# Pooled q and k of two batches summed from transposed tiles, local outputs parked in DRAM, first loads issued by two engines

## The chip, the cores and the metric

The kernel runs on one core of a Trainium2 chip. Its time is device microseconds of one execution, the median of several runs. The core has TensorE (PE in the profile: matmuls, with weight loads as PEld), VectorE (DVE), ScalarE (ACT), GpSimd (POOL) and SyncE (SP, which issues DMAs here; ScalarE can issue them too). All of them run their own instruction streams in program order and wait for one another by semaphores.

## What is computed

Three stages follow each other, all in fp32. B, H, S, D = 4, 8, 576, 64; x has 2304 tokens of 512 columns.

```
q_d, k_d, v_d = mean over 4 neighbouring tokens           # pooled: 144 tokens
out_up    = repeat(softmax(q_d k_d^T / 8) v_d, 4)          # pooled attention, back to 576 tokens
out_local = softmax(q k^T / 8 where |i - j| < 4) v         # banded attention
x = (out_up + out_local) as 2304 x 512
h = x @ w_in;  y = (h * cos(h)) @ w_out                    # first mixture, 2048 wide
yn = y / rms(y) * rms_g
out = (silu(yn @ w_gate) * (yn @ w_val)) @ w_out2          # second mixture, 1536 wide
```

## The kernel before

Every large matrix product is made of three products of rounded parts (a high and a low part of each operand), so TensorE runs at its fp32r rate; ScalarE rounds the high part and VectorE or GpSimd subtracts it to get the low part. The first mixture takes x in nine tiles of 256 tokens. A tile has sixteen chunks of w_in and w_out; two chunks of a tile are a unit (`unit`, L1054 to L1115: matmuls h in L1076, the cosine in L1094 to L1101, high and low part in L1110 to L1112), and `second` (L1142) multiplies by w_out. Units of the tiles 0 and 1 alternate. There are three places for x tiles (`xt`): tile t + 3 can be filled when tile t has been used. Weights come in pieces of 512 KB and are unpacked on ScalarE, VectorE and GpSimd (`w_conv`, L318 to L329).

The attention is the front of this, batch by batch. Of each batch, `block` (L688) does five blocks of 116 tokens for all heads: transposes of q and k (L704), scores with a band mask (L744, L750), softmax (L759 to L772), transposes (L786), the product with v (L812), then the pooled output is added from two PSUM banks, one of each half of the heads (L825), and high and low part go into the x tile (L838, L840). Tokens of the last x tile go to DRAM instead (L844). A block keeps a token `blk` (three of them) and tiles of the five scratch tiles `b2` until its end, and before L812 it waits for the pooled output `od` of its batch.

The pooled attention (`pooled`, L573, a head pair at a time) needs the sums of q, k and v over four tokens. For batch 0 they are made by matmuls from the blocks' own loads (`sums`, L414; `vsums`, L443). For batches 1 to 3, `pq_part` (L500) loads q and k again in ten pieces through a ring `pq`, sums them on GpSimd (L381, L383), transposes the sums (L522) and copies them out (L399, L401); v is loaded and summed in `pv` (L547).

The order of all instructions is worked out by a planner (`Order`, L58 to L191) when the program is built: each step is a generator that yields an engine and an estimated duration, waits for events and takes places from pools; the step that can start earliest goes next, and among those within 0.1 us the one with the smaller due time. The constants in L24 to L55 are such due times and estimates. Where TensorE would be idle in the first 215 us the planner fills in matmuls that compute nothing (`keep_warm`, L241 to L253). What runs on each engine, and in which order, is then fixed.

The start (`start`, L910) sets the order of the first loads by `LOADS` (L40): four weight pieces, five pairs of q and k (q by SP in L861, k by ScalarE in L922, as a step of its own that takes its turn among ScalarE's work), five times the four parts of v (L873, SP), four weight pieces.

Of the kernel before, what the change touches and what calls it, by code (L numbers as in the profile page):

```python
# [194 lines left out]
def fused_kernel(ctx: ExitStack, tc, q, k, v, w_in, w_out, w_gate, w_val, w_out2, rms_g, mask, bmask, out):  # L195
# [20 lines left out]
    for n, c in (("t", 2), ("kk", 2), ("g", 2), ("xt", 3), ("raw", NRAW), ("cv", NCV),  # L216
                 ("blk", 3), ("T", 1), ("blk0", 2), ("b2", 5), ("rq", NQK), ("vb", NV), ("od", 2), ("E", 1), ("qs", NQS), ("vh", 2)):
# [152 lines left out]
    def pq_tiles(b):  # L370

        PQ[b] = [ap.tile([128, 4, 144], F32, tag=f"pqs{w}", name="pqs") for w in range(2)]
# [127 lines left out]
    def pq_part(b):  # L500
# [5 lines left out]
        for w, c, x, m in parts:  # L506
            n = UC[c][1]
            if x == 0:
                qi = yield take("qs")
                qs = ap.tile([128, 4, 64], F32, tag=f"qs{qi}", name="qs")  # L510
# [12 lines left out]
            give("qs", qi)  # L523
# [4 lines left out]
        done(("pq", b))  # L528

# [17 lines left out]
    def pv(b, hp):  # L547
# [3 lines left out]
        p = []  # L551
        for _ in range(2):
            x = yield take("pq")
            p.append(x)
        t = (ap.tile([128, 512], F32, tag=p[0], name="v4").rearrange("p (c x) -> p c x", c=2),
             ap.tile([128, 512], F32, tag=p[1], name="v4")[:, :256])
# [11 lines left out]
        for x in p:  # L568
            give("pq", x)
# [3 lines left out]
    def pooled(b, hp, E=None):  # L573
# [47 lines left out]
        A = ap.tile([128, 3, 144], F32, tag=x, name="at")  # L621
# [66 lines left out]
    def block(b, u, raw, pools):  # L688
# [9 lines left out]
        for w in range(2):  # L698
# [14 lines left out]
            f = (0.125, 1.0)[w]  # L713
# [5 lines left out]
            give("att", "att")  # L719
        qt, kt = T[0][1], T[1][1]  # L720
# [3 lines left out]
        else:  # L724
            if u % 2 == 0:
# [26 lines left out]
        for x, _ in T:  # L752
            give("b2", x)
# [11 lines left out]
        ACT.activation(out=E, in_=E, func=ACTF.Exp)  # L765
# [39 lines left out]
        S_.cur["own"] = held[0][1][:, 0]  # L805
# [47 lines left out]
    def od_free(b):  # L853
        yield wait(("bo", b))
        give("od", od_i[b])

    def raw_dma(t, src, b, u):

        r0 = geo(u)[2]
        yield "SP", 1.75  # L860
# [1050 lines left out]
```

## Time and profile before

| | us |
|---|---|
| median of 3 runs (lowest to highest) | 975.62 (974.25 to 975.81) |
| the profiled execution's own time | 975.6 |
| its span, first to last instruction | 973.8 |
| TensorE busy | 957.8 |
| VectorE busy | 719.7 |
| ScalarE busy | 542.8 |
| GpSimd busy | 254.1 |

The busy times overlap, since the engines run beside each other. A busy TensorE counts the fillers as well. The mean granted TensorE clock of the execution is 0.996.

### The profile page before, as it was taken

Reading aid. Unit: us, or ns where it says so; the run is one execution under the profiler, and the core shown is the slowest. Engines: PE = TensorE matmul, PEld = TensorE weight load, DVE = VectorE, ACT = ScalarE, POOL = GpSimd, SP = SyncE. Lnnn points to the kernel's source line nnn. Section 1 sums busy time; section 2 is a strip of 40 time slices with the busy share of each in tenths; the row PEclk is TensorE's granted clock in tenths of the full one; section 3 lists DMA queues with packets and bytes.
Section 4 is the critical chain, followed back from the end, with each engine's and each line's share of the span. In section 5 each row is a group of like instructions: output and inputs, shape, how many; then the busy total and the mean of one; then the engine's idle time right before and its main releaser. Section 6 shows DMA issues by size and latency. Waiting matters only on the chain.

```text
span 973.8 us, 19223 instructions
## 1 busy us (share of the span) xinstructions
PE 957.8 (98%) x7194; PEld 884.3 (91%) x7194; DVE 719.7 (74%) x1459; ACT 542.8 (56%) x1091; POOL 254.1 (26%) x301
## 2 busy tenths in 40 slices
PE   9989989999999999999999999999999999999998
PEld 9879879888888898888888889999999999999998
DVE  4789985478757866568586789586666678999885
ACT  3667888487768756648565565233223335454432
POOL 3277578345443501100061341000000015200000
PEclk9999999999999999999999999999999999999999
DMA  9649634576796555445432211233222243444432
GB/s 204 201 98 295 177 87 130 150 193 169 206 232 175 152 167 157 146 155 206 152 123 77 74 44 53 62 93 98 82 71 78 63 152 123 142 159 151 132 119 77
DMA packets 157678, 132.16 MB, mean 136 GB/s; under 512 B 71824, under 2 KB 131600, under 8 KB 157584
## 3 DMA queue, kind: packets, MB, share of 16 engines
q1 hardware_dynamic: 152384, 129.61, 44.8%
q10 hardware_dynamic: 5200, 1.31, 0.7%
q8 instruction: 57, 0.93, 0.4%
q14 instruction: 37, 0.30, 0.1%
HBM read 94.71 MB, written 36.18 MB: 134 GB/s over the span
## 4 chain that ended last, share of the span: by engine, by line
PE 84%; DVE 9%; ACT 2%; SPq 2%; issue 2%; DMA 1%; DVEq 0%; ACTq 0%
PE gvp L1565 26%; PE y L1142 18%; PE h L1076 16%; PE o L1818 13%; PE bav L812 2%; PE btr L704 1%; SPq L861 1%; PE bs L750 1%; PE yt L1470 1%; PE avp L648 1%; DVE rawwa L324 1%; PE sps L592 1%; DMA rawwa<-in_moe_w_out 1%; DVE bt L825 1%; PE bat L786 1%
## 5 line engine op out<-in xcount | busy, mean ns | idle before, releaser
L1565 PE MATMUL gvp<-xc,wc 128*128 128x384 f32 x1296 | 231.3, 335 | 0.0
L1565 PEld LDWEIGHTS gvp<-xc,wc 128*128 128x128 f32 x1296 | 225.5, 188 | 0.2
L1636 DVE TENSOR_TENSOR tmp<-gvp,tmp 128x384 f32<-128x384 f32 x180 | 99.3, 554 | 55.3 <-PE gvp L1565 52.0
L1076 PE MATMUL h<-big,wwa 128*128 128x256 f32 (+1 forms) x756 | 124.8, 317 | 2.9 <-DVE t L1101 2.2
L1076 PEld LDWEIGHTS h<-big,wwa 128*128 128x128 f32 x756 | 107.5, 190 | 13.2 <-DVE t L1101 2.7
L1818 PE MATMUL o<-wo,wc 128*128 128x256 f32 x972 | 118.4, 279 | 0.0
L1818 PEld LDWEIGHTS o<-wo,wc 128*128 128x128 f32 x972 | 115.7, 190 | 0.0
L1142 PE MATMUL y<-wwa,big 128*128 128x512 f32 x432 | 109.5, 399 | 0.0
L1142 PEld LDWEIGHTS y<-wwa,big 128*128 128x128 f32 x432 | 78.6, 188 | 16.8 <-issue 0.8
L1096 DVE SCALAR_TENSOR_TENSOR t<-kk,h 128x512 f32<-128x512 int32 x72 | 49.1, 682 | 45.9 <-ACT kk L1094 45.7
L1076 PE MATMUL h<-big,wwb 128*128 128x256 f32 (+1 forms) x504 | 82.9, 316 | 0.0
L1142 PE MATMUL y<-wwb,big 128*128 128x512 f32 x324 | 81.0, 397 | 0.0
L1076 PEld LDWEIGHTS h<-big,wwb 128*128 128x128 f32 x504 | 72.1, 190 | 6.4 <-issue 0.2
L1094 ACT ACTIVATE kk<-h 128x512 int32<-128x512 f32 x72 | 42.7, 593 | 58.0 <-PE h L1076 57.9
L1142 PEld LDWEIGHTS y<-wwb,big 128*128 128x128 f32 x324 | 59.2, 188 | 12.2 <-issue 0.4
L1101 DVE TENSOR_TENSOR t<-h,t 128x512 f32<-128x512 f32 x72 | 49.3, 686 | 23.2 <-ACT t L1099 22.8
L1702 POOL TENSOR_TENSOR wt<-wo 128x256 f32<-128x256 f32 x10 | 9.7, 975 | 208.5 <-DMA wo<-wfs 183.1
L1099 ACT ACTIVATE t<-t,cst 128x512 f32<-128x512 f32 x72 | 51.9, 721 | 15.1 <-DVE t L1096 14.6
L1627 ACT ACTIVATE tmp<-gvp 128x384 f32<-128x384 f32 x36 | 17.7, 492 | 75.2 <-PE gvp L1565 73.0
L1761 ACT ACTIVATE wc<-ut 128x512 fp32r<-128x512 f32 (+1 forms) x60 | 34.3, 584 | 42.2 <-DVE ut L1747 25.2
L1110 ACT ACTIVATE big<-t 128x512 fp32r<-128x512 f32 x72 | 45.1, 628 | 17.6 <-DVE t L1101 17.2
L1672 DVE TENSOR_TENSOR tmp<-tmp 128x384 f32<-128x384 f32 x72 | 43.7, 608 | 11.9 <-ACT tmp L1660 11.4
(192 smaller groups left out, 1729.8 us busy)
## 6 DMA issues: line engine op xcount, KB each, us to landing
us<-tmp SPq DMA_DIRECT2D x72, 192.0 KB, 2.0
uf<-us SPq DMA_DIRECT2D x48, 256.0 KB, 2.9
rawwa<-in_moe_w_out SPq DMA_DIRECT2D x22, 512.0 KB, 4.4
wfs<-rawwa SPq DMA_DIRECT2D x36, 256.0 KB, 2.6
rawwa<-in_moe_w_gate SPq DMA_DIRECT2D x12, 512.0 KB, 4.6
rawwa<-in_moe_w_val SPq DMA_DIRECT2D x12, 512.0 KB, 4.6
wf<-wfs SPq DMA_DIRECT2D x12, 512.0 KB, 4.2
rawwa<-in_moe_w_in SPq DMA_DIRECT2D x11, 512.0 KB, 5.6
```

The costliest lines, as they stand in the source:

```text
L1076: PE.matmul(h[:, w_ * ci:w_ * ci + w_], a[:, ksl], x_at(x, kk), start=m == 0, stop=m == 11)
L1094: ACT.activation(out=kk, in_=h, func=ACTF.Copy, scale=INV2PI, bias=0.25)
L1096: DVE.scalar_tensor_tensor(out=t, in0=kk, scalar=TWOPI, in1=h, op0=ALU.mult, op1=ALU.subtract)
L1099: ACT.activation(out=t, in_=t, func=ACTF.Sin, scale=-1.0, bias=cst[:, 0:1])
L1101: DVE.tensor_tensor(out=t, in0=h, in1=t, op=ALU.mult)
L1110: ACT.activation(out=gh, in_=t, func=ACTF.Copy)
L1142: PE.matmul(y[j][b], g[:, tsl], a, start=(first and ci == 0 and i == 0), stop=(last and c == 15 and i == 2))
L1565: PE.matmul(bank, w[:, a, kk], xc[:, x, b, kk], start=first and i == 0, stop=i == 5, skip_group_check=True)
L1636: DVE.tensor_tensor(out=half(o), in0=a, in1=half(b), op=ALU.add)
L1672: DVE.tensor_tensor(out=half(v), in0=half(v), in1=half(sl), op=ALU.mult)
L1761: ACT.activation(out=o[:, 0], in_=src, func=ACTF.Copy)
L1818: PE.matmul(b[m][1][:, l], u[0][x][:, j, l], w[:, y, k], start=(p == 0 and l == 0 and i == 0), stop=(p == C3 - 1 and i == 2), skip_group_c ...
```

## The change

- For the third and the fourth batch, q and k are no longer loaded a second time for the pooled attention. When a block has transposed its q and k, `token_sums` sums four neighbouring columns of the transposed tile on VectorE, straight into the pooled tile; the transposed tile is given back when both this and the scores are done. The factor of q changes from 1/8 to 1/128 to suit both uses, and the local softmax's exponential scales by 16. Only the second batch still goes through `pq_part`; its ring has two tiles (`pqs01`, `pqs11`, which later hold the third batch's sums), and its sums take a scratch tile `b2`. The summed v has tiles of its own.
- The product of a block with v goes to one PSUM bank for both halves of the heads, and one instruction takes it out. For the first batch this adds the pooled output as before. For the others it is a plain copy (ScalarE or VectorE), stored to DRAM (`loc`), and the block ends there without having waited for the pooled output. A new step `join` waits for the pooled output and for the x tile's place, loads the parked block, adds the pooled output (GpSimd or VectorE) and goes on as before (`to_x`). The low part there may be taken by VectorE too.
- ScalarE issues the five k loads of the first batch at the very start, and one half of each v load (ten DMAs). SP issues the other ten. Three weight pieces go ahead of q instead of four, and five follow v.
- The constants of the planner (due times, biases, estimates) change.

```diff
-PH = 50
-BD = (-40, -45)
+D1 = (-170, -260, -40)
+DJ, BU = (-200, 4)
+BD = (-200, -45)
-RAWT = 1.8
-SD, PD, VD = (-200, -20, -20)
-LOADS = (("w", 4), ("r", 5), ("v", 5), ("w", 4),)
+RAWT = 1.1
+SD, PD, VD = (-40, -200, -20)
+LOADS = (("w", 3), ("r", 5), ("v", 5), ("w", 5),)
+KACT, VACT = 5, (0, 1, 2, 3, 4)
+XLB = 0.3
-SLACK = 2.5
+SLACK = 2
-DS = 0
+DS = 2
-TP = 5
-WD = 0.004
-NQS = 1
+TP = 8
+WD = 0.005
-DU = {"conv": 20, "pool": -320, "blk": -170}
+DU = {"conv": 20, "pool": -300, "blk": -200}
...
-    S_.pool("ax", ["pq1"])
-    S_.pool("pq", ["pq0", "pq2"])
+    S_.pool("pq", ["pqs01", "pqs11"])
...
+    def token_sums(b, u, w, x, o):
+        yield wait(("pq", 1) if b == 2 else ("pS", 1))
+        if b not in PQ:
+            pq_tiles(b)
+        _, n, _, off = geo(u)
+        yield "DVE", 0.6
+        DVE.tensor_reduce(out=PQ[b][w][:, :, 29 * u:29 * u + n // 4], in_=o[:, :, off:off + n].rearrange("p a (j r) -> p a j r", r=4), axis=AX.X, op=ALU.add)
+        count(("pq", b), 10)
+        if count2(("Tu", b, u, w), 2):
+            give("b2", x)
...
-            f = (0.125, 1.0)[w]
+            f = (2.0 ** -7, 1.0)[w]
...
+            if b > 1:
+                S_.add(token_sums(b, u, w, x, o), S_.cur["due"], slack=0.0)
...
-        ACT.activation(out=E, in_=E, func=ACTF.Exp)
+        ACT.activation(out=E, in_=E, func=ACTF.Exp, scale=16.0)
...
-        yield wait(("od", b))
-        held = []
-        for e in range(2):
-            yield take("att", 1 - e)
-            i = yield take("bank")
-            held.append((i, bank_tile(i, [128, 4, 116], "bav")))
+        if b < 1:
+            yield wait(("od", b))
+        yield take("att")
+        i = yield take("bank")
+        bav = bank_tile(i, [128, 4, 116], "bav")
...
-                    PE.matmul(held[e][1][pr, a, 58 * s:58 * s + m], VB[v_i][pr, s, a], ba[pr, a, 64 * s:64 * s + m], start=True, stop=True)
+                    PE.matmul(bav[pr, a, 58 * s:58 * s + m], VB[v_i][pr, s, a], ba[pr, a, 64 * s:64 * s + m], start=True, stop=True, skip_group_check=True)
...
+        if b:
+            _, e = yield [("ACT", 0.58, t0), ("DVE", 0.64, t0, None, 0.3)]
+            if e == "ACT":
+                ACT.activation(out=bx, in_=bav[:, :, :n], func=ACTF.Copy)
+            else:
+                DVE.tensor_copy(out=bx, in_=bav[:, :, :n])
...
+        if b:
+            yield "SP", 0.8
+            SP.dma_start(loc[b, u, :, :4 * n], bx.rearrange("p a q -> p (a q)"))
+            give("b2", x_i, S_.now())
+            give("blk", 0)
+            done(("loc", b, u), S_.now())
+            S_.add(join(b, u), T0 + T1 * (S * b + i0) / TT + DJ)
+            return
...
+    def join(b, u):
+        i0, n, _, _ = geo(u)
+        yield wait(("loc", b, u))
+        yield wait(("od", b))
+        for ti in range((S * b + i0) // TT, min(NTILE - 2, (S * b + i0 + n - 1) // TT) + 1):
+            yield wait(("xt", ti))
+        x_i, bx = yield from t2k()
+        bx = bx[:, :4 * n].rearrange("p (a q) -> p a q", a=4)
+        yield "SP", 0.8
+        SP.dma_start(bx.rearrange("p a q -> p (a q)"), loc[b, u, :, :4 * n])
+        _, e = yield [("POOL", 1.2), ("DVE", 0.66, None, None, 0.5)]
+        y = bx.rearrange("p a (j r) -> p a j r", r=4)
+        (POOL if e == "POOL" else DVE).tensor_tensor(out=y, in0=y, in1=pooled_at(b, i0, n), op=ALU.add)
+        count(("bo", b), 5)
+        yield from to_x(b, u, bx)
...
+    def v_act(u, x):
+        for s in range(2):
+            yield "ACT", 0.38
+            v_window(0, u, x, 0, s, ACT)
+        S_.cur["t"] += 3.5
+        count(("rv", 0, u), 2)
...
     def blk_due(b, u):
         if b == 0:
             return T0 + BD[0] if u < 3 else T0 + T1 + BD[1]
-        return T0 + T1 * (S * b + 116 * u) / TT + DU["blk"]
+        if b == 1:
+            return T0 + T1 * (S * b + 116 * u) / TT + D1[0]
+        return T0 + T1 * S * b / TT + BU * u + DU["blk"]
...
+        rt = [early(("raw", u), [128, 2, H, D]) for u in range(5)]
+        for u in range(KACT):
+            yield "ACT", 0.38, (0, None)
+            ACT.dma_start(rt[u][:, 1], k[0, :, geo(u)[2]:geo(u)[2] + 128, :].rearrange("h t d -> t h d"))
...
-                yield from load_v(0, u, x)
+                if u in VACT:
+                    S_.add(v_act(u, x), -250.0)
+                yield from load_v(0, u, x, (1,) if u in VACT else (0, 1))
```

## Rows read from the trace of the kernel before

**Rows 1.** The page's head: span, then each engine's busy us, share and instructions.

```profile
span 973.8 us, 19223 instructions
PE 957.8 (98%) x7194; PEld 884.3 (91%) x7194; DVE 719.7 (74%) x1459; ACT 542.8 (56%) x1091; POOL 254.1 (26%) x301
```

**Rows 2.** Groups by line and shape: busy us, mean ns | idle before; the fillers.

```profile
L253 PE MATMUL warm<-ident 128*128 128x128 f32 x198 | 28.2, 295 | 1.4 <-POOL ident masks.py:199 1.4
```

**Rows 3.** Busy us of each engine by stage, over the first 500 us.

```profile
core 0: us, PE busy (x) PEld busy (x) DVE busy (x) ACT busy (x) POOL busy (x), PEclk, DMA share, GB/s
0.00:24.00 24.00, 22.63 (x210) 22.13 (x210) 10.84 (x25) 9.52 (x21) 9.32 (x18) 1.00 0.92 203
0.00:14.00 14.00, 12.64 (x99) 12.64 (x99) 6.23 (x17) 5.98 (x12) 7.48 (x16) 1.00 0.91 232
14.00:34.00 20.00, 19.75 (x225) 18.69 (x224) 8.70 (x19) 8.44 (x20) 3.65 (x3) 1.00 0.77 145
34.00:56.00 22.00, 19.68 (x268) 15.85 (x266) 19.29 (x49) 16.87 (x58) 7.24 (x8) 0.92 0.50 169
80.00:140.00 60.00, 55.60 (x459) 48.83 (x458) 54.92 (x86) 51.13 (x89) 44.83 (x46) 1.00 0.65 186
140.00:200.00 60.00, 59.70 (x514) 53.42 (x513) 32.44 (x60) 42.03 (x90) 35.19 (x45) 1.00 0.46 128
200.00:500.00 300.00, 299.26 (x2404) 258.94 (x2403) 209.46 (x434) 204.81 (x395) 82.20 (x112) 1.00 0.59 175
```

**Rows 4.** Timeline, all engines, 0 to 40 us: start, us, engine, line, [idle before].

```profile
14.75 17.80 SPq L873 DMA_DIRECT2D vb<-in_v  x20
...
22.22 0.40 ACTq L922 DMA_DIRECT2D raw<-in_k  x1
...
22.72 0.67 ACT L326 ACTIVATE wwa<-rawwb 128x512 fp32r<-128x512 f32 x1 [5.08 <-DMA vb<-in_v]
...
29.64 0.97 PE L426 MATMUL pq<-sel,raw 128*128 128x28 f32 x8
```

**Rows 5.** Timeline of TensorE, 48 to 82 us: the first units, and four transposes.

```profile
62.75 4.87 PE L1076 MATMUL h<-big,wwa 128*128 128x256 f32 x36
67.46 0.60 PE L522 MATMUL trq<-ident,qs 128*64 128x128 f32 x4
67.82 1.67 PE L1076 MATMUL h<-big,wwa 128*128 128x256 f32 x12
```

**Rows 6.** Groups of VectorE by line and shape, whole span.

```profile
L825 DVE TENSOR_TENSOR bt<-bav,od 64x464 f32<-64x464 f32 x32 | 20.4, 638 | 5.8 <-PE bav L812 5.2
...
L767 DVE TENSOR_REDUCE bst<-bt 128x8 f32<-128x512 f32 x15 | 10.2, 681 | 5.7 <-ACT bt L765 5.6
```

**Rows 7.** Timeline of VectorE, 50 to 75 us.

```profile
56.45 3.99 DVE L825 TENSOR_TENSOR bt<-bav,od 64x464 f32<-64x464 f32 x6 [0.64 <-PE bav L812]
```

**Rows 8.** Timeline of TensorE, 36 to 48 us: 64-row matmuls.

```profile
38.77 1.20 PE L592 MATMUL sps<-pqs 64*72 64x144 f32 x16
...
46.14 1.69 PE L652 MATMUL avp<-at,vs 64*64 64x144 f32 x24
```

**Rows 9.** Instructions on the tile trq: duration ns min/median/max, first and last start.

```profile
L522 PE MATMUL trq<-ident,qs x54: 270/272/299, 67.5 to 296.9; 128*64 128x128 f32 x54
```

**Rows 10.** Busy us by stage, columns as in rows 3.

```profile
52.50:56.00 3.50, 3.50 (x68) 2.90 (x64) 2.46 (x5) 3.43 (x8) 1.67 (x2) 0.51 0.02 5
```

**Rows 11.** Timeline of TensorE, 118 to 192 us.

```profile
119.70 1.21 PE L592 MATMUL sps<-pqs 64*72 64x144 f32 x8
...
159.72 0.71 PE L592 MATMUL sps<-pqs 64*72 64x144 f32 x8
...
173.98 0.90 PE L648 MATMUL avp<-at,vh 128*128 128x144 f32 x6
...
190.98 1.20 PE L1076 MATMUL h<-big,wwa 128*128 128x256 f32 x8
```

**Rows 12.** The chain that ended last: start us, us, what; a block's product.

```profile
176.26 1.07 PE bav L812 x32
```

More of the change, by code (lines that the diff above doesn't have):

```diff
@@ L370, in pq_tiles @@
     def pq_tiles(b):
-        PQ[b] = [ap.tile([128, 4, 144], F32, tag=f"pqs{w}", name="pqs") for w in range(2)]
+        PQ[b] = [ap.tile([128, 4, 144], F32, tag=f"pqs{w}{int(b == 2)}", name="pqs") for w in range(2)]
     od_t, od_i, ring = {}, {}, {}
@@ L508, in pq_part @@
             if x == 0:
-                qi = yield take("qs")
-                qs = ap.tile([128, 4, 64], F32, tag=f"qs{qi}", name="qs")
+                qi, qs = yield from t2k()
+                qs = qs[:, :256].rearrange("p (u d) -> p u d", u=4)
             yield wait(("pq", b, w, c, x))
@@ L550, in pv @@
         vh = VH[vi]
[L551 to L556, printed above, removed]
+        p = yield take("pv")
+        t = (ap.tile([128, 512], F32, tag="pva", name="v4").rearrange("p (c x) -> p c x", c=2),
+             ap.tile([128, 256], F32, tag="pvb", name="v4"))
         yield from pv_load(b, hp, *t)
@@ L620, in pooled @@
         x = yield take(a)
-        A = ap.tile([128, 3, 144], F32, tag=x, name="at")
+        A = ap.tile([128, 3, 144], F32, tag=x, name="at") if a == "a" else x
         yield take("att")
@@ L724, in block @@
         else:
[L725 removed]
+            if u == 4:
+                pass
+            elif u % 2 == 0:
                 pl = yield take("pqp")
@@ L819, in block, with pooled_at, to_x @@
         x_i, bx = yield from t2k()
[L820 to L829 removed]
+        bx = bx[:, :4 * n].rearrange("p (a q) -> p a q", a=4)
[5 more added lines that the diff above has]
+                DVE.tensor_copy(out=bx, in_=bav[:, :, :n])
+        else:
+            yield "DVE", 0.64, t0
+            DVE.tensor_tensor(out=bx.rearrange("p a (j r) -> p a j r", r=4), in0=bav[:, :, :n].rearrange("p a (j r) -> p a j r", r=4),
+                              in1=pooled_at(b, i0, n), op=ALU.add)
+        give("bank", i)
+        give("att", "att")
+        if b:
[6 more added lines that the diff above has]
+            return
+        count(("bo", b), 5)
+        yield from to_x(b, u, bx)
+        give("b2", x_i, S_.now())
+        give("blk", 0)
+    loc = dram.tile([B, 5, 128, 464], F32, name="loc")
+    def pooled_at(b, i0, n):
+        return od_t[b][:, :, i0 // 4:(i0 + n) // 4].unsqueeze(3).to_broadcast([128, 4, n // 4, 4])
+    def to_x(b, u, bx):
+        i0, n, _, _ = geo(u)
         at = 0
@@ L934, in start @@
         S_.add(select(early("sel", [128, 1024])), -60)
-        for x in range(3):
+        t = early(("E2", 2), [128, 2, 512])
+        P["E2", 2] = (t, pl["E2", 2])
+        give("ax", t[:, 1, :432].rearrange("p (c q) -> p c q", c=3))
+        for x in range(2):
             give("pqp", pl["E2", x])
@@ L1002, in free_E2 @@
         yield wait(("E2f", x))
+        if x == 2:
+            yield wait(("od", 0))
         give(P["E2", x][1][2], P["E2", x][1])
@@ L1009, in pool_ctl @@
         for b in range(1, B):
-            due = T0 + T1 * (9 * b / 4) + DU["pool"]
+            due = T0 + T1 * (9 * b / 4) + (D1[1] if b == 1 else DU["pool"])
             S_.due(due)
-            if b > 1:
-                yield wait(("pS", b - 1))
-            S_.add(pq_part(b), due, slack=SLACK)
-            yield wait(("pq", b))
+            if b == 1:
+                S_.add(pq_part(b), due, slack=SLACK)
+                yield wait(("pq", b))
+                due += D1[2]
             for hp in range(4):
-                S_.add(pv(b, hp), due + PH + 5.0 * hp)
-                S_.add(pooled(b, hp), due + PH + 5.0 * hp, slack=SLACK)
+                S_.add(pv(b, hp), due + 5.0 * hp)
+                S_.add(pooled(b, hp), due + 5.0 * hp, slack=SLACK)
+            yield wait(("pS", b))
     G = {}
```

66 lines of the change are left out of this document (30 added, 36 removed).

## The prediction

> **What bounds the kernel now.** I read the page's totals first. TensorE is busy for 957.8 of 973.8 us, so nothing else can be the bound over the whole span [rows 1]. That number hides the fillers, so the second view is the group of line 253: 198 matmuls "warm" that compute nothing, 28.2 us [rows 2]. The third view cuts the span into stages [rows 3]. From 140 to 500 us TensorE idles 1.0 us (59.70 of 60, 299.26 of 300): there only TensorE work that disappears is worth anything, and work of VectorE, ScalarE, GpSimd and the queues is free as long as it keeps ahead. Before 140 us it is different. In 0 to 14 us the DMA engines are full (0.91) and TensorE runs fillers only. In 14 to 34 us VectorE works 8.70 of 20 us: it waits for data. In 34 to 56 us it works 19.29 of 22, in 80 to 140 us 54.92 of 60, and TensorE loses 4.4 us there (55.60 of 60): VectorE is the bound of that stretch.
>
> The timeline of the first 40 us says what the data wait for [rows 4]. Behind the q loads SP issues the twenty v loads over 17.80 us. ScalarE issues the k loads from the middle of its own program; the fourth goes out at 22.22 us, after ScalarE had sat 5.08 us until a v load landed (the bracket of its next row). So the last pair of q and k is first used at 29.64 us, and the pooled scores of batch 1, which need all five, begin after that. The first unit of the mixture starts at 62.75 us [rows 5].
>
> The profiled execution took 975.6 us for a span of 973.8, so 1.8 us lie around it; the median of the three timed runs is 975.62, the same. The sum below is made against 975.6.
>
> **The change, part by part.** (Batches are counted from 0 as in the code; the title's batches 3 and 4 are 2 and 3.)
>
> *Early loads.* Ahead of the last q, k load there now are the band mask (0.07 MB), three weight pieces of 0.52 instead of four, and ten loads of 0.26: 4.26 MB. In the first 24 us the DMA engines moved 203 GB/s [rows 3], so these land after 21.0 us, plus about 2 us from the span's start to the first bytes: 23 us, against 29.64 us. The twenty v loads (1.31 MB, 6.4 us) follow, with ten issues on SP (half of 17.80, 8.9 us) and ten on ScalarE. So the data come 6.7 us earlier. How much of it reaches the first unit? VectorE has 11.3 free us in 14 to 34, but only 2.7 in 34 to 56. I bound the gain by 0 (the full stretch swallows it) and 6.7 (all passes), and take 4, nearer to the upper end, because it is the idle stretch that is filled. The five k issues at 0.40 us are 2 us of ScalarE, hidden: it works 5.98 of the first 14 us, and the weight pieces that they delay are read only by the first unit, 40 us later. The ten v issues are 4 us in 14 to 34, where ScalarE works 8.44 of 20. Each of the ten can wait as the k load did, and behind it then stand the evictions of the sums and of the transposes, for which TensorE waits. One wait of 5.08 us goes and one may come: 0, with 5.1 on both sides.
>
> The Trainium skill speaks against this part: "DMA: Bandwidth & Descriptors", section "Issuing engines are not separate DMA queues", says that issuing from several engines saves only the sequencer's time for the issue, since the same 16 DMA engines do the work. By that alone the 4 us would be 0 and the sum 970.4. The trace agrees for the first 14 us (share 0.91) but not for 14 to 34 us, where the share is 0.77 and the last k load was held up by its issue.
>
> *One bank for the local product of a block.* The two half evictions of 0.638 us (64 partitions each [rows 6]) become one over 128 partitions with the same columns, so the same 0.64 us. For batch 0 the six halves of blocks 0 to 2 stand back to back on VectorE for 3.99 us [rows 7], just ahead of the first unit; three remain: 2.0 us gained on the path. Bounds: 0 (VectorE fills it with weight conversions) and 3.2 (all ten halves to five). I take 2.0.
>
> Both halves of the block's matmuls now write one bank. 64-row matmuls that write one bank are in the trace: L652 takes 1.69 us for 24, L592, which writes two banks, 1.20 us for 16, with the same 144 columns [rows 8]: 70 and 75 ns each. So I cost the one bank at nothing. The Trainium skill says otherwise, "TensorEngine Tiling (Array Packing)", section "Gotcha 1: PSUM Pressure": different row tiles cannot access one bank at the same time. By it the pairs would run one after the other (a rival, below); the two rows speak against it.
>
> *Pooled q, k of batches 2 and 3.* 36 of the 54 transposes L522 go [rows 9]. The pair of starts 67.46 and 67.82 gives 0.36 us for four, 0.09 us each [rows 5]: 3.2 us of TensorE, in 165 to 297 us, where it is saturated. This is the surest term. Their 20 loads, 40 GpSimd additions and 18 evictions go as well. New are 20 reductions on VectorE; the nearest row is L767, 681 ns for 512 columns [rows 6]: 13.6 us, hidden beside TensorE in 140 to 500 us (VectorE 242 of 360 us busy [rows 3]). If that cover went, they would cost up to their 13.6 us. Each holds its transposed tile, one of five scratch tiles, until it has run; blocks queue for those.
>
> *Parked outputs.* For 15 blocks: a copy out of the bank (0.64 us, on ScalarE or VectorE), a store, a load, an addition (0.64 us on VectorE), in place of 30 half additions of 0.638 us. VectorE and ScalarE come out even; SP gets 30 issues of about 0.6 us, 18 us in 360. Gained: a block no longer stands on its product until the pooled output of its batch is there, so that blocks can fill TensorE's idle 4.4 us in 80 to 140 us. Since VectorE is the bound there and a block loads VectorE too, I take 0 of 0 to 4.4. Lost: after the pooled output comes a load instead of a product. That is hidden if the x tile is early; where it isn't is the third rival.
>
> *Priorities and due times* reorder everything and have no row. I take 0; the clock shows their size: after pauses of TensorE in the head the granted clock is 0.51 from 52.5 to 56.0 us (1.2 GHz instead of 2.4) [rows 10], so such a pause costs about 1.7 us beyond itself, and one avoided gives that back.
>
> Sum: 975.6 - 4 - 2.0 - 3.2 = 966.4 us.
>
> **The rivals.**
> (a) *The head's gain is lost.* VectorE is full from 34 to 140 us, and what it does there (weights, blocks) doesn't shrink; the mixture starts earlier and then waits. For: 54.92 of 60 us. Against: its idle 11.3 us in 14 to 34. Only 3.2 and a part of the 2.0 stay: 971.4.
> (b) *Nothing.* One more wait of 5.08 us on ScalarE in the head eats the 4 us, and the reorder gives gaps back. Within 2 us of 975.6.
> (c) *Slower: the third x tile is late.* Unit 16, the first on x tile 2, starts at 190.98 us, and the local products that this tile needs can only come after the last pooled product of batch 1 at 173.98: it is just in time now [rows 11]. The pooled scores of batch 1 come one head pair every 13.3 us (119.70 to 159.72, three steps). Its q, k loads now have two ring tiles instead of three and take a scratch tile of the blocks for their sums. If that costs one step of the chain and TensorE has run out of blocks, 13.3 us are lost: 966.4 + 13.3 = 979.7. It decides as soon as the last pooled product of batch 1 comes later than about 174 - 9 = 165 us plus what blocks TensorE still has. Against: the 15 blocks of batches 1 to 3 are no longer bound to the pooled output and can fill it.
> (d) *One bank serialises the pairs.* A block's product takes 1.07 us now [rows 12]; with its pairs one after the other at most twice that, 20 blocks: 21.4 us, 987.8. The trace speaks against it, as said.
>
> **How the numbers follow.** Forecast 0.55, (a) 0.17, (b) 0.10, (c) 0.14, (d) 0.04. The likeliest is 966.4 us. Its own ends: 975.6 - 6.7 - 3.2 - 3.2 - 4.4 = 958.1 with all at their best, and 970 to 971 with the wait of 5.1 us on ScalarE. The range that leaves out 2 in 10 takes in (a), (b) and most of (c): 958.5 to 979.5. A measurement of this kernel can't tell less than about 0.2%, 2 us, from no change. Faster: 0.55 + 0.17 = 0.72; same 0.10; slower 0.18.
>
> **What would show it.** Early loads: the k issues in the first 5 us of ScalarE's queue, the last pooled sum's matmul at about 23 us, the first unit at about 57 us instead of 62.75. If the matmul comes early and the unit doesn't, (a). The bank: the block's 32 matmuls still at about 1.07 us; at 2 us it is (d). The transposes: 18 of L522. Parked outputs: no idle of TensorE of over 2 us between 140 and 500 us; a hole in front of the first unit on x tile 2 is (c). A bracket of several us behind ScalarE's v issues is (b). Wrong would be a time above 973.6 us, or one below 958.

## The result, and the profile after

The changed kernel takes 987.92 us (median, 987.22 to 988.23) against 975.55 us for the kernel before: ratio 1.0129, 95% interval 1.0114 to 1.0144, slower by 12.4 us where 9.2 us less were forecast. The profiled execution took 987.2 us for a span of 985.4 (before: 975.6 for 973.8 [rows 1]), so 11.6 us of span are to be found. The head of the page of the changed kernel:

```profile
span 985.4 us, 19034 instructions
PE 957.9 (97%) x7110; PEld 884.3 (90%) x7110; DVE 727.5 (74%) x1476; ACT 550.1 (56%) x1084; POOL 222.4 (23%) x252
```

TensorE has the same busy time as before with 84 matmuls less; a busy time says nothing about the clock at which it was worked off. The stages of [rows 3], in the changed kernel:

```profile
0.00:14.00 14.00, 12.64 (x99) 12.65 (x100) 1.86 (x11) 1.59 (x2) 4.88 (x14) 1.00 0.92 214
14.00:34.00 20.00, 11.10 (x113) 10.24 (x112) 5.98 (x11) 8.04 (x20) 3.88 (x3) 0.61 0.98 221
34.00:56.00 22.00, 22.00 (x160) 20.18 (x161) 12.26 (x38) 9.71 (x41) 3.91 (x6) 0.74 0.32 86
80.00:140.00 60.00, 54.18 (x483) 47.85 (x482) 52.11 (x83) 47.65 (x82) 40.05 (x42) 0.97 0.72 213
140.00:200.00 60.00, 57.37 (x544) 49.59 (x543) 49.87 (x90) 48.02 (x88) 33.89 (x41) 1.00 0.49 128
200.00:500.00 300.00, 297.14 (x2344) 257.32 (x2343) 210.69 (x436) 208.31 (x390) 56.72 (x72) 1.00 0.60 182
```

Three things stand out. In the first 14 us ScalarE works 1.59 us instead of 5.98, and VectorE 1.86 instead of 6.23. From 14 to 34 us TensorE works 11.10 us instead of 19.75, at a granted clock of 0.61. From 34 to 56 us it is busy without a gap (22.00 of 22) and yet gets through 160 matmuls instead of 268: the clock is 0.74. The two stages hold (0.39 x 20 + 0.26 x 22) x 2 = 27 us at 1.2 GHz. The timeline of ScalarE, 0 to 24 us, gives the cause of all three:

```profile
2.78 14.99 ACTq L990 DMA_DIRECT2D raw<-in_k  x5
17.82 1.21 ACT L1030 ACTIVATE bm<-bf 64x64 fp32r<-64x64 f32 x5 [15.48 <-DMA raw<-in_q]
19.06 0.65 ACT L323 ACTIVATE rawwa<-rawwa 128x512 f32<-128x512 f32 x1
```

and the same five issues by their line (duration ns min/median/max, first and last start):

```profile
L990 ACTq DMA_DIRECT2D raw<-in_k x5: 374/375/435, 2.8 to 17.4; - x5
```

One issue takes 375 ns, but the five take 14.99 us: they start at 2.78, 6.02, 10.11, 13.15 and 17.40 us. The trace shows what each stood for. In this program the loads of SP and of ScalarE share eight completion semaphores (a semaphore tells that a load has landed), and in the trace each of the five issues starts within 0.03 us of the landing of the load that had its semaphore before: at 2.76 us (the mask), 6.00 and 10.09 (weights), 13.13 and 17.38 (two q loads). Everything else of ScalarE stands behind: the mask copies L1030, the first weight L323 (19.06 us), the evictions. VectorE waits for that weight:

```profile
19.75 0.69 DVE L325 SCALAR_TENSOR_TENSOR rawwa<-rawwa 128x512 int32<-128x512 int32 x1 [13.29 <-ACT rawwa L323]
```

and TensorE waits twice (timeline of TensorE; the row of 64.12 us is three blocks' product with v, the last row the first unit, [rows 5] before):

```profile
18.40 0.79 PE L757 MATMUL bs<-bm,ident_r 128*128 128x256 f32 x2 [2.42 <-ACT bm L1030]
25.66 1.14 PE L763 MATMUL bs<-bt 64*64 64x64 f32 x32 [6.47 <-ACT bt L724]
...
64.12 2.98 PE L825 MATMUL bav<-bt,vb 64*64 64x58 f32 x96
...
69.44 6.24 PE L1152 MATMUL h<-big,wwa 128*128 128x256 f32 x48
```

The first unit starts 6.7 us later than before (62.75). From there to the end of the span it is 916.0 us, against 911.1 before: another 4.9 us. In the stages from 80 to 500 us TensorE idles 11.3 us, where it idled 5.4 before [rows 3]. Of the rest, the transposes are down from 54 to 18 as meant [rows 9], and a block's product isn't slowed: a matmul takes 218 ns at the median, and 96 of them follow one another in 2.98 us, so 32 in 0.99, where the kernel before takes 1.07 [rows 12] (instructions on the tiles trq and bav):

```profile
L523 PE MATMUL trq<-ident,bt x18: 271/272/273, 78.6 to 124.9; 128*64 128x128 f32 x18
...
L825 PE MATMUL bav<-bt,vb x640: 213/218/262, 64.1 to 361.7; 64*64 64x58 f32 x144, 64*64 64x54 f32 x16
```

### The profile page after: what moved, and what is told of

It reads as the page before. It is cut to its first block, busy times and chain, and to the rows that moved or that the text cites. A ratio compares the mean times of both kernels' runs of the same rounds, so it can differ in the third digit from the quotient of the medians.

```text
span 985.4 us, 19034 instructions
## 1 busy us (share of the span) xinstructions
PE 957.9 (97%) x7110; PEld 884.3 (90%) x7110; DVE 727.5 (74%) x1476; ACT 550.1 (56%) x1084; POOL 222.4 (23%) x252
## 4 chain that ended last, share of the span: by engine, by line
PE 83%; DVE 8%; ACT 3%; DMA 2%; issue 2%; SPq 1%; DVEq 0%; ACTq 0%
PE gvp L1641 26%; PE h L1152 18%; PE y L1218 17%; PE o L1894 13%; PE bav L825 2%; PE btr L713 1%; PE pq L427 1%; PE bs L763 1%; DVE rawwa L325 1%; PE avp L657 1%; PE sps L601 1%; PE bat L800 1%; DMA raw<-in_q 1%; DMA y<-ysc 1%; SPq L914 1%
## 5 line engine op out<-in xcount | busy, mean ns | idle before, releaser
L1170 ACT ACTIVATE kk<-h 128x512 int32<-128x512 f32 x72 | 42.7, 595 | 49.6 <-PE h L1152 48.2
L1218 PEld LDWEIGHTS y<-wwb,big 128*128 128x128 f32 x324 | 59.1, 188 | 11.9 <-issue 0.4
L1703 ACT ACTIVATE tmp<-gvp 128x384 f32<-128x384 f32 x36 | 17.7, 492 | 76.1 <-PE gvp L1641 76.1
```

The lines of the kernel that those rows point to most:

```text
L1170: ACT.activation(out=kk, in_=h, func=ACTF.Copy, scale=INV2PI, bias=0.25)
L1218: PE.matmul(y[j][b], g[:, tsl], a, start=(first and ci == 0 and i == 0), stop=(last and c == 15 and i == 2))
```

## The experiments

Two theories stood against each other at first. One: the early k issues block ScalarE, and with it the head; all else is small. The other: the parts behind the head (parked outputs, blocks drawn forward, v issues on ScalarE) cost the time. The kernel before was run beside each kernel on the same chip; its medians were 974.8 to 975.7 us. "Order" means the list of instructions of each engine. The planner works with booked prices and writes it anew for every edit that changes a price, a wait or a ring; an edit that only changes what a step issues keeps it. In the runs below that are said to keep the order, the traces show the same list for TensorE, VectorE, ScalarE and GpSimd, apart from the edit itself.

**The early k issues alone, in the kernel before.** Every engine's order is that of before except for the five issues.

```diff
-        def load_k(t, u): yield "ACT", 0.3; ACT.dma_start(t, k[...])
+        for u in range(5):
+            yield "ACT", 0.38, (0, None)
+            ACT.dma_start(rt[u][:, 1], k[...])
```

> The kernel before with one thing alone: the five k loads at ScalarE's front. Theory: 984 to 992 us, ScalarE idle over 12 us behind the issues, the first unit some 7 us later than 62.8. Rival (order and parking cost it): within 3 us of 975.6.

Measured 988.67 us, ratio 1.0120 (1.0064 to 1.0176). Timelines of ScalarE and TensorE:

```profile
2.84 12.28 ACTq L923 DMA_DIRECT2D raw<-in_k  x5
15.16 1.22 ACT L957 ACTIVATE bm<-bf 64x64 fp32r<-64x64 f32 x5 [12.83 <-issue]
...
25.10 1.14 PE L750 MATMUL bs<-bt 64*64 64x64 f32 x32 [5.78 <-ACT bt L715]
...
80.43 0.38 PE L1076 MATMUL h<-big,wwa 128*128 128x256 f32 x1
```

This one edit gives a loss as large as that of the whole change, with the same pattern and no other part of the change present. So the issues suffice. The profiled execution (993.2 us; the four lie at 984 and at 994) loses it all in the head: the first unit starts 17.7 us late, and from there to the end it takes 911.0 us, as in the kernel before. The head is hit harder here than in the changed kernel (6.7 us), so that the two losses are alike in size is partly chance.

**k issued by SP, the rest as changed.** SP puts each k behind its q; ScalarE issues half of v only.

```diff
-KACT, VACT = 5, (0, 1, 2, 3, 4)
+KACT, VACT = 0, (0, 1, 2, 3, 4)
```

> The changed kernel, with the k loads issued by SP, each behind the q load of its block; the v loads stay halved. Theory: ScalarE is free in the head as well, 970 to 976 us; the last pooled sum of batch 0 before 30 us, since SP does nothing else. Rival (order and parking): 982 to 988 us.

Measured 974.25 us (970.12 to 977.47), ratio 0.9985 (0.9968 to 1.0002): the 13.7 us to the changed kernel are gone, and no gain on the kernel before can be told. Timelines of ScalarE and TensorE, then two stages:

```profile
2.96 0.26 ACT L1030 ACTIVATE bm<-bf 64x64 fp32r<-64x64 f32 x1 [0.62 <-DMA bf<-band_mask]
...
25.26 0.97 PE L427 MATMUL pq<-sel,raw 128*128 128x28 f32 x8
...
55.08 6.36 PE L1152 MATMUL h<-big,wwa 128*128 128x256 f32 x48 [0.15 <-ACT big L875]
...
81.14 1.96 PE L825 MATMUL bav<-bt,vb 64*64 64x58 f32 x32 [3.92 <-DVE bt L809]
```

```profile
56.00:80.00 24.00, 21.04 (x199) 18.80 (x197) 22.40 (x31) 19.27 (x34) 19.22 (x18) 1.00 0.82 252
80.00:140.00 60.00, 55.67 (x494) 49.51 (x495) 45.16 (x80) 48.82 (x89) 36.26 (x43) 0.94 0.58 169
...
200.00:500.00 300.00, 296.88 (x2285) 256.13 (x2284) 206.57 (x436) 201.32 (x381) 55.68 (x70) 1.00 0.57 175
```

With a free ScalarE the head comes as forecast: last pooled sum at 25.3 us (forecast 23), first unit at 55.08 (forecast 57), 7.7 us earlier than before. But from there to the end it takes 917.7 us instead of 911.1, so 6.6 of the 7.7 us are given back, and most of it at once: the fifth unit (the 97th of the matmuls h) starts at 89.8 us, before at 91.3. Between them a block's product waits 3.92 us for VectorE, which works 22.40 of 24 us from 56 to 80, and the clock falls behind that wait (0.94 over 80 to 140 us). Between the first and the fifth unit TensorE idles 1.6 us more than in the kernel before and runs 2.5 us more of fillers; the rest of the 6.2 us is half clock and block work, which this order brings forward. That looks like rival (a): the mixture starts earlier and then waits for VectorE. It isn't shown to be that alone, since the order is a new one. Later TensorE idles 3.1 us in 200 to 500 us instead of 0.7, with 4 us less work to do.

**The k issues in ScalarE's turn again, and no v on ScalarE.** Two runs, each one part undone in the changed kernel: k as steps between ScalarE's other work as before; all v by SP.

```diff
-        for u in range(KACT): yield "ACT", 0.38, (0, None); ACT.dma_start(...)
+        S_.add(load_k(t[:, 1], u), 0.0, 0.0)
```

> The changed kernel, with the five k loads of the first batch issued as before (each a step that takes its turn among ScalarE's work) instead of all at ScalarE's front. Theory (ScalarE stands 15.48 us behind the k issues, TensorE starves and its clock falls for 27.3 us): the loss of the head goes, 970 to 975 us, first unit before 63 us, no half clock of over 10 us. Rival (the parked blocks and the new order cost it: unit 16 comes at 208.8 instead of 191.0 us): at most 5 us better, 982 to 988 us.

```diff
-KACT, VACT = 5, (0, 1, 2, 3, 4)
+KACT, VACT = 5, ()
```

> The changed kernel, with all twenty v loads issued by SP; the k loads stay at ScalarE's front. Theory: the k issues are the cause, so most stays: 983 to 988 us; the v issues on ScalarE are worth up to 5 us (its waits of 1.86 and 2.56 us between 37 and 43 us). Rival (the v halves are the cause, since they now land at 49.5 us): 975 to 980 us.

Measured 996.05 us (ratio 1.0211, 1.0196 to 1.0226) and 995.72 (1.0206, 1.0184 to 1.0227). Each takes one suspected cost away and is 8 us slower than the changed kernel. Without the v issues the k issues stand as long (15.20 us), so v is not the cause; the brackets behind the v issues of the changed kernel are 1.86 and 2.56 us. With k in turn ScalarE stands three times (3.98, 3.88 and 2.72 us), and a hole opens late (timelines of TensorE and GpSimd):

```profile
405.03 0.79 PE L1151 MATMUL h<-big,wwa 128*128 128x512 f32 x1 [5.80 <-ACT big L875]
...
404.58 2.44 POOL L901 TENSOR_TENSOR bt<-bt,od 128x464 f32<-128x464 f32 x2 [24.18 <-DMA bt<-loc]
```

A parked output is loaded and added too late for its x tile, and the unit waits 5.80 us: rival (c) in another place. In the changed kernel itself no such hole is there. That taking costs away made the kernel slower was the first sign that the order is a cause of its own.

**The wait taken out, with the order kept.** The five issues stay at ScalarE's front. Only the copy of the identity matrix, which stood ahead of them and waits for GpSimd, goes behind them; so the k loads are the first of all and three find a free semaphore.

```diff
-    ACT.activation(out=ident_r, in_=ident, func=ACTF.Copy)
...
         yield "ACT", 1.0
+        ACT.activation(out=ident_r, in_=ident, func=ACTF.Copy)
```

> The kernel before with the five k loads at ScalarE's front and the copy of the identity matrix behind them; every engine's order is else that of before, so this is the run with early k issues in the kernel before (988.7) with most of the wait taken away. If the wait is what cost 13 us: mask copies by 8 us instead of 15.2, first unit 56 to 64 us instead of 80.4, end 971 to 977. If early k loads cost by pushing q and the weights back: first unit over 68 us, end 981 or more.

> The changed kernel with one instruction moved: ScalarE's copy of the identity matrix, which stands ahead of its five k issues and itself waits for GpSimd, goes behind them, just ahead of the mask copies. The k issues then come first of all loads and three of the five find a completion semaphore that nothing holds; the order of every engine is otherwise that of the changed kernel. If ScalarE's 14.99 us at the issues are the cause: mask copies by 8 us instead of 17.8, first unit 55 to 61 us instead of 69.4, end 974 to 979. If the loads themselves or the order behind them are the cause (early k traffic ahead of the weights, a poor order from 60 us on): first unit over 64 us or the gain lost again, end 984 or more.

In the kernel before: 978.15 us (977.01 without one execution of 991.34, which the ratio leaves out), ratio 1.0036 (1.0014 to 1.0059), 10.5 to 11.7 us less than with the full wait. Timelines of ScalarE and TensorE:

```profile
0.73 7.59 ACTq L922 DMA_DIRECT2D raw<-in_k  x5
...
31.38 0.97 PE L425 MATMUL pq<-sel,raw 128*128 128x28 f32 x8
...
63.00 0.39 PE L1075 MATMUL h<-big,wwa 128*128 128x256 f32 x1
```

So the wait is what cost. And a second thing: the last q, k pair is in at 22.3 us here (29.5 in the kernel before, by the trace's landings), yet the last pair's first sum stands at 31.38 us (29.64 before [rows 4]) and the first unit at 63.00. The first pair, for its part, lands 2.2 us later (15.8 us, before 13.7), and from its first sum at 15.95 us (13.79 before) TensorE works through its list, fillers included, without a wait. So the list, and not the landing of the last pair, sets when that pair is used: data 7 us earlier bring nothing in an order that was written for the later ones.

In the changed kernel: 985.32 us, ratio 1.0094 (1.0060 to 1.0129), with a wide spread of 978.7 to 989.7. The profiled execution is the fastest: first unit at 61.48 us, and 915.4 us from there to the end (timeline of TensorE).

```profile
61.48 6.26 PE L1151 MATMUL h<-big,wwa 128*128 128x256 f32 x48
```

So the wait moved the head by 8 us as theory one said, but only in that execution did the gain reach the end whole. By the medians it is 2.6 us of 12.4, and the two intervals overlap: at the end of the changed kernel the price of the wait is not shown by this run. The other four, of which there is no trace, show a lower mean clock (0.979 to 0.983, against 0.993).

**The clock behind the wait.** Fillers in the changed kernel just ahead of the first block's mask matmul, where TensorE stands for ScalarE; the order is kept, and ScalarE stands as long.

```diff
+        if b == 0 and u == 0:
+            for _ in range(70):        # second run: 37
+                PE.matmul(held[0][1][:, 0:2]..., ident, ident, start=True, stop=True)
         for _, t in held:
             PE.matmul(t, ident_r, bm[...])
```

> The changed kernel with 70 further filler matmuls on TensorE (128x128 of the identity, into a bank whose contents the next matmul overwrites) just ahead of the first block's mask matmul, where TensorE stands 2.42 us and then 6.47 us for ScalarE; the order of every engine is otherwise that of the changed kernel and ScalarE stands at its k issues as there. At 118 ns a filler they last from about 16 to 24 us, before the 25.66 us at which the next work is ready. If the granted clock of one half over 27.3 us is what costs: the half-clock stretch is gone or under 10 us, end 976 to 981. If the wait itself costs (everything behind the mask copies late): clock at full speed, end still 984 to 988.

> The run with 70 fillers again, with 37: each was two matmuls of 113 ns, so that the 70 lasted to 31.6 us, 6 us past the time at which the next work was ready; 37 end at about 24.3 us, before it. ScalarE's stand at the k issues stays. If the granted clock of one half behind the wait was the larger part: last pooled sum by 36 us, first unit 60 to 63 us (69.4 in the changed kernel, 66.6 with 70 fillers), end 978 to 983. If the wait alone fixes the head: first unit over 65 us, end 985 or more.

With 70: 987.02 us (ratio 1.0111, 1.0087 to 1.0135), but a filler is two passes of 113 ns, so that they held TensorE to 31.6 us. With 37: 984.87 us (1.0101, 1.0084 to 1.0117); timeline of TensorE and two stages:

```profile
16.90 8.51 PE L758 MATMUL bs<-ident 128*128 128x128 f32 x74
25.16 0.48 PE L760 MATMUL bs<-bm,ident_r 128*128 128x256 f32 x2
25.70 0.69 PE L766 MATMUL bs<-bt 64*64 64x64 f32 x32
```

```profile
14.00:34.00 20.00, 19.95 (x231) 19.47 (x229) 8.61 (x18) 8.91 (x23) 3.90 (x3) 1.00 1.02 228
34.00:56.00 22.00, 20.95 (x180) 17.81 (x179) 14.64 (x40) 13.54 (x52) 5.93 (x7) 0.84 0.36 81
```

The same 32 matmuls take 0.69 us instead of 1.14, the last pooled sum starts at 35.4 us instead of 42.7, the first unit at 64.8 instead of 69.4, and the end gains 3.1 us. Both expectations were too sharp. With 37 fillers 6.8 us at half clock are left, from 34.2 to 41.1 us, and TensorE has no wait from 14 us to there; why the clock fell is open. So the 20.5 us at half clock that went are worth 7.3 us at the sums, 4.6 at the first unit and 3.1 us of the 12.4 at the end. How the rest divides between the wait and the 4.9 us behind the first unit these runs don't show.

**The single bank.** First re-planned, in the kernel before:

```diff
-        for e in range(2): yield take("att", 1 - e); i = yield take("bank"); held.append(...)
+        yield take("att"); i = yield take("bank"); bav = bank_tile(i, [128, 4, 116], "bav")
...
-        for e in range(2): yield "DVE", 0.63; DVE.tensor_tensor(out=bx[pr...], in0=held[e][1][pr...], ...)
+        yield "DVE", 0.64, t0; DVE.tensor_tensor(out=bx[:...], in0=bav[:...], ...)
```

> The kernel before with one edit: both head halves of a block's attention-times-v in one PSUM bank, evicted by one VectorE instruction of 128 partitions instead of two of 64. The prediction's term: 20 evictions of about 0.64 us less, of which the middle of the bounds, 2.0 us, reaches the end: 973.6, the chain's 32 matmuls at 1.07 us as before. Against it: off the path, 975.6 within 0.2%. Rival (d), matmuls of the two halves serialised in one bank: 987.8 and a chain of about 2 us.

Measured 986.65 us, ratio 1.0127 (1.0108 to 1.0145): 11.9 us slower, close to the price of rival (d), and yet a matmul of the product takes 218 ns as before and TensorE's losses are spread over 60 to 560 us. So the same edit was run with the order kept: the planner still books two banks and two evictions, and the second one issues nothing.

```diff
             yield "DVE", 0.63, t0 if e else None
-            DVE.tensor_tensor(out=bx[pr...], in0=held[e][1][pr...], ...)
+            if e == 0:
+                DVE.tensor_tensor(out=bx[:...], in0=held[0][1][:...], ...)
```

> The kernel before with the single bank and the one eviction of 128 partitions, but with the planner's steps and prices kept (it still books two evictions; the second one issues nothing), so that every engine runs the same order as before and only 20 VectorE instructions of about 0.63 us are gone. If the 12 us of the run with one bank came from its re-planned order and not from the bank: 973 to 976, and the prediction's term of -2.0 us (0 to 3.2) is read from it. If one bank in itself costs (matmuls that serialise, banks held longer): 980 or more.

Measured 974.18 us, ratio 0.9982 (0.9972 to 0.9992), the one kernel here whose interval lies below the kernel before. VectorE's groups by shape, and the matmuls on the tile:

```profile
L825 DVE TENSOR_TENSOR bt<-bav,od 128x464 f32<-128x464 f32 x16 | 10.2, 640 | 7.6 <-PE bav L812 7.3
...
L812 PE MATMUL bav<-bt,vb x640: 214/218/312, 54.5 to 429.1; 64*64 64x58 f32 x144, 64*64 64x54 f32 x16
```

16 evictions of 640 ns in place of 32 of 638 [rows 6], matmuls as before. In the profiled executions the first unit starts 0.3 us earlier than in the kernel before (62.43 us), and the wait of the next block's product for ScalarE is 0.72 us instead of 2.32. The 12 us of the run before it are the price of its order.

**Orders of the same work.** So the planner was given one wrong price at a time, with the work untouched:

```diff
-            yield "PE", 0.2 * n      # first nudge: transposes of a pooled sum
+            yield "PE", 0.21 * n
-RAWT = 1.8                           # second: a k load
+RAWT = 1.9
-            yield "DVE", 0.63, ...   # third: half eviction
+            yield "DVE", 0.66, ...
```

> The kernel before with one number of the planner changed that touches no work: the price it books for a transpose of a pooled sum is 0.21 us instead of 0.20. The same instructions are issued, in another order in many places. If the order that the planner writes is good or bad by chance on the scale of the differences seen (12 us with one bank re-planned): it moves by 4 us or more, either way, between 970 and 990. If orders of this planner are all about as good: 974 to 977.5, and the 12 us need another cause.

> The kernel before with another planner's number nudged that touches no work: a k load of the first batch is booked at 1.9 us of SP instead of 1.8. The order differs in 136 rows of TensorE's list. If the order before is a picked one among many of uneven quality: slower again, 978 to 990. If the first nudge (986.5) was an exception: 974 to 977.5.

> A third nudge of the kernel before that touches no work: the eviction of a half block of attention outputs is booked at 0.66 us of VectorE instead of 0.63. The order differs in 56 rows of TensorE's list, fewer than with the two nudges that gave 986.5 and 989.3. If every new order is worse than the one that the kernel before has: 978 to 990. If small differences leave the time: 974 to 977.5.

Measured 986.49 us (ratio 1.0106, 1.0090 to 1.0123), 989.26 (1.0123, 1.0094 to 1.0153) and 977.14 (1.0016, 1.0007 to 1.0026); they differ from the order before in about 200, 136 and 56 rows of TensorE's list (a row is a run of like matmuls). The first one's stages and longest waits of TensorE:

```profile
140.00:200.00 60.00, 57.51 (x487) 50.84 (x486) 35.44 (x64) 40.45 (x79) 28.82 (x39) 1.00 0.46 133
200.00:500.00 300.00, 293.83 (x2365) 251.83 (x2364) 203.86 (x420) 195.27 (x380) 72.24 (x103) 0.99 0.56 167
```

```profile
PE y L1142 <- POOL big L1112: 3.4, 3, 1.7
PE h L1076 <- DVE t L1101: 2.7, 3, 1.3
```

Where the kernel before idles 1.0 us (59.70 of 60, 299.26 of 300 [rows 3]), this one idles 8.7 us, in pieces of 1 to 2 us at hand-overs between the engines. The same with the changed kernel and k on SP, under the first nudge and another one (the sum of a block's exponentials booked at 0.76 us instead of 0.75):

> The changed kernel with k issued by SP, and the same nudge that moved the kernel before to 986.5: a transpose of a pooled sum is booked at 0.21 us instead of 0.20. Without the nudge it took 974.2. If its order too is one draw among many: it moves by 4 us or more, to 978 to 990 if 974.2 was a good draw, to 965 to 970 if it was a poor one. If the changed content makes the order robust: 972 to 977.

> As the run before this one, with another nudge: the sum of a block's exponentials is booked at 0.76 us of VectorE instead of 0.75. Together with it: if the work that the change takes from TensorE (4 us) is worth something in itself, the draws of the changed kernel with k on SP lie lower than the nudged ones of the kernel before (986.5 and the other nudge), by about 4 us; if not, they lie in the same place.

Measured 987.62 us (1.0117, 1.0096 to 1.0138) and 974.58 (0.9993, 0.9975 to 1.0011). What the nudges cost lies behind the first unit: from there to the end it is 923.6, 929.9 and 912.4 us for the three of the kernel before. Where its order was kept, it is 911.0 and 911.5 us (early k issues, and with the wait taken out). Of the eleven kernels with the change's work eight lie at 915.4 to 918.4, with ScalarE standing at its front or not, and three at 922.3 to 930.0 (k in turn, no v on ScalarE, the first nudge). So orders of one and the same work lie 14 us apart, with and without the change: 975.4, 977.1, 986.5, 989.3 for the work of before, 974.2, 974.6, 987.6 for that of the change with k on SP. No gain of 4 us can be told from these seven.

**Three further orders.** k by SP in the kernel before; all q, k and v by SP in the changed kernel; the changed kernel with the whole head of before.

```diff
-                S_.add(load_k(t[:, 1], u), 0.0, 0.0)
+                yield from raw_dma(t[:, 1], k, 0, u)
```

> The kernel before with one edit: the five k loads of the first batch are issued by SP, each behind its q, instead of by ScalarE in turn with its other work. Theory 1 (rival (a) in place): a freed ScalarE brings the first unit some 7 us earlier, as in the changed kernel with k on SP (55.1 us against 62.8), but the stretch from 60 to 200 us is paced by VectorE's block work and gives it back: first unit 54 to 57, unit 12 within 2 us of 163.2, end 974 to 976. Theory 2: the gain is lost in the changed kernel by its own later parts (blocks moved earlier, joins), and the kernel before would carry it to the end: unit 12 at 156 to 158, end 967 to 970.

> The changed kernel with the five k loads and all v loads issued by SP, so that ScalarE issues none of the first batch's loads. With k on SP and half of v on ScalarE it was 974.2. If what hurts is ScalarE standing at its issues until an earlier load has landed, the four or so us at the v issues go too: first unit 53 to 55 us, end 970 to 974. If SP's longer queue delays v by more than ScalarE gains: last v after 45 us, first unit as with half of v on ScalarE or later, end 974 to 979.

> The changed kernel with the head of the kernel before: k issued by ScalarE in turn, all v by SP, the load order, due times of the first batch and the planner's price of a k load as before. What is left of the change is pooled q, k of batches 2 and 3 from the transposed tiles, the single bank, the parked outputs and the planner's constants of the later batches. If the head alone spoilt the change: first unit 62 to 64 us, TensorE's own work 3 to 4 us shorter than before, end 970 to 973. If the parked outputs and the earlier blocks have a price of their own (late third x tiles, TensorE waiting with a lower granted clock from 60 to 450 us, as with k in turn): end 976 to 985 in spite of the old head.

Measured 974.54 us (0.9996, 0.9987 to 1.0006), 975.76 (1.0011, 1.0002 to 1.0020) and 978.35 (1.0041, 1.0026 to 1.0056). In the profiled execution of the first, the first unit comes 3.5 us earlier than before (59.24 us) and the end 1.7. The third has TensorE's shorter work, the old head, and idles 5.5 us in 200 to 500 us instead of 0.7. Read against the scatter above, the three say only that none of them is far from the kernel before.

## Why the prediction was wrong, step by step

*Early loads, -4 us.* The first half of the step held: the data were forecast complete at 23 us and landed at 24.0 (29.5 before). Two sentences failed behind it. "The five k issues at 0.40 us are 2 us of ScalarE, hidden" took an issue's duration for its price: the duration is right (375 ns), the stand is 14.99 us. And "One wait of 5.08 us goes and one may come: 0, with 5.1 on both sides" counted one wait for ten v issues and none for the five k. The bracket of 5.08 us [rows 4] had shown the mechanism, an issue on ScalarE that stands until another load has landed; it applied to each issue that was moved in front of loads still on their way, and what was queued behind those was not the weights alone but the mask copies and all evictions of the sums. The forecast's own numbers gave a wider bound: the waits end when loads issued ahead land, and those it had complete at 23 us, so up to some 20 us, not 5.1.

The other half was also mis-sized. I took 29.64 us as a wait for data whose end moves the first unit. With the data 7 us earlier and the order kept, the first unit stayed (63.00 against 62.75). Its order, fillers included, was written for the later data; only a new order drew the first unit to 55.08 us, and there 6.2 of the 7.7 us were gone by the fifth unit. By the Trainium skill's "Issuing engines are not separate DMA queues" ("DMA: Bandwidth & Descriptors") the 4 us were 0. The run with the order kept gives that 0 too, though not for the page's reason, since the data did come earlier; with k issued by SP alone the kernel before takes 974.54 us, no longer than with two issuing engines, which agrees with the page as far as a new order can tell.

*The clock.* "Such a pause costs about 1.7 us beyond itself" was read from a stretch of 3.5 us [rows 10]. Here 27 us were granted at 1.2 GHz; 20.5 of them taken away gave 7.3 us at the last pooled sum and 3.1 us at the end.

*One bank, -2.0 us, bounds 0 and 3.2.* The size was right: ratio 0.9982 (0.9972 to 0.9992), which is 0.8 to 2.7 us less, with the order kept. The path was not: the 2.0 us were to come just ahead of the first unit, which starts only 0.3 us earlier, so that the number fits is partly luck. Rival (d) is refuted: 218 ns per matmul in one bank and in two, and 32 of them in 0.99 and 1.07 us. The Trainium skill ("TensorEngine Tiling (Array Packing)", "Gotcha 1: PSUM Pressure") differs here from the measurement, and the measurement decides.

*Pooled q, k, -3.2 us.* The transposes went as forecast, 54 to 18. From the start of one such transpose to the next start is 0.11 us at the median, so 36 of them are 3.9 us of TensorE's work, a little more than the 3.2. That it reached the end is shown by no run: every kernel that has it also has a new order, and these scatter by 14 us.

*Parked outputs, 0.* No idle of TensorE of over 2 us between 140 and 500 us in the changed kernel (longest 1.3 us), so right there. Of rival (c) the first half came about: the last pooled product of batch 1 starts at 193.23 us instead of 173.98, and unit 16 at 208.78 instead of 190.98. The second half did not: TensorE had other work and no hole opens in front of that unit. With k in turn one did, at another tile: 5.80 us.

*Priorities and due times, 0.* This is the second step that failed. "They reorder everything and have no row" was true, and for that very reason 0 needed bounds. Nudges without any work give +2.0, +11.1 and +13.6 us on the medians. The 4.9 us that the changed kernel loses behind its first unit lie well inside that. Whether they come from the order alone or from a part of the change is open: no run has the change's work in the order of before, since its steps are others.

*The rivals.* (a) fits what was seen as soon as ScalarE was free (k on SP): 974.25 us, where it was priced at 971.4. (b) named the right mechanism, ScalarE standing at issues, with a third of the price and at v instead of k. The 11.6 us of span are 6.7 ahead of the first unit and 4.9 behind it; the first are the k issues, shown by the run with nothing else and by the ones with the wait taken out, and the cause of the second is open. Two slips of the text: its end "970 to 971" is 966.4 + 5.1 = 971.5, and "the pooled scores of batch 1, which need all five" are those of batch 0.

## What to carry to other kernels

Price a DMA issue that is moved onto a compute engine by the landing of the loads ahead of it, not by its own duration, and list everything that stands behind it in that engine's order. Where a program writes the order, measure first how far null changes of its prices move the time; a gain smaller than that scatter can be tested only with the order kept. If an early load is to help, look whether its reader stands idle for it, or only comes late in the list.

## What the runs showed of the hardware

- An issue of 375 ns stood up to 3.9 us (from 13.5 to 17.40 us), until a load of SP's queue had landed (17.38 us), with eight completion semaphores for the loads of SP and ScalarE together. As the first loads of all, three of the five go out without a wait (five issues in 7.59 us instead of 12.28).
- With TensorE standing 2.42 and 6.47 us around 20 us, the granted clock was 1.2 GHz for 27 us, from 18.2 us, at the end of the first stand, to 45.5 us; from 25.66 us on TensorE had been busy without a gap. With 37 fillers in the same place it stayed at 1.00 from 14 to 34 us, with 70 to 56 us. It can fall without a stand just ahead of it, as the 6.8 us from 34.2 us on with 37 fillers show.
- 64-row matmuls of both halves of the heads that write one PSUM bank follow one another no slower than with two: 96 in 2.98 us, against 32 in 1.07.
- Three of the kernels that issue k early repeat badly (978.7 to 989.7, 983.8 to 994.2 and 975.6 to 991.3 us, where the kernel before stays within 973.4 to 978.0); the changed kernel itself, with the same stand, doesn't (987.2 to 988.2). Why is open.
